# The skip term of eleven output blocks made by GpSimd: five of them leave TensorE, six leave VectorE

## The chip, the cores and the metric

The kernel runs on one core of a Trainium2 chip. The metric is the device time of one execution in microseconds (us). Three runs of the kernel before took 286.35, 286.96 and 289.43 us (median 286.96).

A core has these engines, each with its own queue of instructions in a fixed order: TensorE (PE: matmuls into the eight PSUM banks; the loads of its weights are shown as PEld), VectorE (DVE), ScalarE (ACT), GpSimd (POOL), and SyncE (SP), which here issues every DMA. An instruction whose inputs aren't there holds all that stand behind it on its engine.

## What is computed

x has 2048 tokens of 512 channels. The reference, cut to what matters here:

```python
g = _sigmoid((x * gate_w).sum(-1, keepdims=True))
a = _A_ref(x, A_wq, A_wk, A_wv, A_wo, A_beta)     # attention with memory, ends in o @ wo
b = _B_ref(x, B_A_re, ..., B_Dskip)               # y = ifft(fft(u) * fft(K)) + u * Dskip
return g * a + (1 - g) * b
```

So each output row is a sum of three terms: the attention output o times wo, the long convolution y, and the skip term x times a channel's constant (Dskip and the convolution's first tap). The kernel keeps (1 - g) apart as a scale for each token (omg4T) and has the rest of the gate inside o.

## The kernel before, in words

The whole program is a graph of operations. `op` records one with its engine, a function that emits it, and the tiles it reads and writes; `S.dma` records a DMA on SyncE, `S.evac` an eviction from PSUM that either ScalarE (L229, or L232 with a scale) or VectorE (L230, L233) can do. All matmuls go through one helper, L713, so the profile shows that line for all of them. `ORDER` (L382) is the written-out list of all operations: each entry is an operation's number, and behind slashes the buffer of each tile that this operation is the first to use; an "a" or "v" puts an eviction on ScalarE or VectorE. `replay` (L238) walks the list: each engine gets its operations in that order, and a tile that takes a buffer also takes, as `prev`, all users of the tile that had the buffer before. `emit` (L267) turns these into semaphore waits in front of the instruction. So both the place in the list and the buffer number decide what waits for what.

The tail of the program has three strands:

- The last attention heads: scores, an exponential by ScalarE (L1197, L1244), masks by VectorE (L1256), and a normalisation (L1158 to L1161). For token segments 0 to 2 a head group's result goes to DRAM and is read back transposed by SyncE (L1309; the last such read is oT2.3, operation 840). For segment 3, TensorE transposes it and it is evicted (oT3.3, on VectorE, L230); the eviction also waits for the read oT2.3 to land.
- The convolution (`conv`, L1413): for each of 32 frequencies a matmul, a product on VectorE (L1494), a matmul, an eviction to a V buffer (L1505, one of four) and a copy by DMA into V2 (L1506, "V copy" below). V copies 25, 26, 28, 29, 30 and 31 are the late ones.
- `finals` (L1510): sixteen output blocks b of 128 x 512, in a hand-mixed order.

A block's matmuls are fin (three of the four head groups' 128x512 matmuls), fir (one, half the convolution), fih (one, the fourth head group) and fis (one, the other half of the convolution). fih needs all four segments' fourth head group, oT2.3 and oT3.3 among them; fis needs all V copies.

- Blocks 8 to 15 keep their PSUM bank from fin to fis ("held"). Their skip term is part of fin: four matmuls of 128 columns of x against a diagonal matrix (L1532 to L1534). Their output is a scaled eviction by ScalarE (L232) or VectorE (L233): in this kernel 9 and 14 on VectorE, the others on ScalarE.
- Blocks 0 to 7 give the bank back. Their skip term is made on VectorE in an SBUF tile Ab (xD, L1528) from x rows that a DMA brings (xr0, xr2, xr4, xr6: one load for two blocks, 256 KB, two buffers); VectorE adds the first part of the sum (spl, L1550), and later the second part gives the output (out, L1564).

Two blocks share a store (L1567). TensorE takes the tail's matmuls in this order of blocks: fin1, fin6, fin7, fin10, fin3, fin5, fin0, fin2, fin8, fir8, fih8, fin11, fin14, fir14, fih10, fih14, fis14, fis8 and so on, between the last attention and convolution matmuls up to oT3.3; fin13 to fis13 end it. fih8 is the first fih.

SyncE's order there is: the load of wo, xr0, a convolution constant (CD29), xr6, a swap (X31), V copy 19, the read oT1.3, V copy 28, the other half of the swap, xr2, CD30, V copies 27, 20, 31, 26, the read oT2.3, xr4, V copies 25, 29, 30, then the eight stores.

Of the kernel before, what the change touches and what calls it, by code (L numbers as in the profile page):

```python
# [8 lines left out]
BF16 = mybir.dt.bfloat16  # L9
F32 = mybir.dt.float32  # L10
# [455 lines left out]
1687/0/1 1688a 1742 840 1682/0 1683/4/0 1006/2 1007 1776 1689/3 1008 1724/2 1727 1702/0 1703 1718/6 1690/1/3 1719
1026/5 1027v 1764/2 1765 1766 1780/5 1732/1 1657 1684a 1740/0 1743 1797/4 1685 1798 1777 1691a 1692 1799 1704 1800/0
1801v 1767/1 1733/1 1753/1 1721/0 1778/2 1769/7 1717/3 1720 1712/4 1713/3 1714 1722/4 1723 1768a 1779a 1728/2 1729
1770 1781 1782 1783 1784a 1734/6 1771 1772 1773v 1802/3 1803 1804 1785 1774 1754/5 1755 1735 1737/4 1730 1760/0 1761
1736 1705/5 1706 1707 1744/7 1745/2 1786/1 1762 1731 1715 1763 1805 1806a 1807 1787 1788 1789/1 1746 1738 1739 1791/6  # L470
# [71 lines left out]
def build_graph(nc, es, A_x, A_wq, A_wk, A_wv, A_wo, A_beta, B_A_re, B_A_im, B_B_re, B_B_im,  # L542
                B_C_re, B_C_im, B_log_dt, B_Dskip, gate_w, out):
    S = Sched(nc, es)
    ap = S.ap
    op = S.op
    x = A_x[0]
# [32 lines left out]
    G2T = cload(G2c, "G2", BF16, 60)  # L580
# [5 lines left out]
    diagT = S.keep(1024, BF16)  # L586
# [6 lines left out]
    omg4T = S.keep(64, F32)  # L593
# [53 lines left out]
    a = H2 + 16384  # L647
# [10 lines left out]
    a = T0  # L658
# [10 lines left out]
    a = H0  # L669
# [3 lines left out]
    a = H1  # L673
# [836 lines left out]
    def finals(V2, k0):  # L1510
        o3 = [oTp[(s_, hg)] for s_ in range(4) for hg in range(3)]
        o4 = [oTp[(s_, 3)] for s_ in range(4)]
        ou = None
        xr = {}
        for b4 in range(16):
            held = b4 not in SPILL
            S.key = k0 + b4
            P = S.ps()
            Ab = None if held else Tile(AbPs[SPILL[b4]], F32)
            if not held:  # L1520
                if b4 % 2 == 0:
# [6 lines left out]
                op("DVE", ("V1s", 512), lambda e, b4=b4, Ab=Ab, T=xr[b4]: e.scalar_tensor_tensor(  # L1528
                    ap(Ab, n=512), ap(T, (b4 % 2) * 512, n=512), ap(omg4T, b4, n=1), ap(DbT, n=512), ALU.mult, ALU.mult), r=[xr[b4], omg4T, DbT], w=[Ab], key=k0 - 10 + b4)
# [12 lines left out]
            def fv(e, P=None, b4=b4, q=0, last=False):
                return mm(e, ap(P, n=512), ap(G2T, q * 128, n=128), ap(V2[q], b4 * 512, n=512), False, last)
            S.tag = "fin%d" % b4
            op("PE", c_pe("F", 512), f1, r=o3 + (xTT + [woT, diagT] if held else [woT]), w=[P])
            S.tag = "fir%d" % b4
            op("PE", c_pe("F", 512), lambda e, P=P, fv=fv, held=held: fv(e, P, q=0, last=not held), r=[G2T, V2[0]], pw=[P])
            if not held:
                S.tag = "spl%d" % b4
                op("DVE", ("V1s", 512), lambda e, P=P, Ab=Ab, b4=b4: e.scalar_tensor_tensor(ap(Ab, n=512), ap(P, n=512), ap(omg4T, b4, n=1), ap(Ab, n=512), ALU.mult, ALU.add),  # L1550
                   r=[P, omg4T], w=[Ab])
                P = S.ps()
            S.tag = "fih%d" % b4
            op("PE", c_pe("F", 512), lambda e, P=P, f2=f2: f2(e, P), r=o4 + [woT], **({"pw": [P]} if held else {"w": [P]}))
            S.tag = "fis%d" % b4
            if b4 % 2 == 0:
                ou = Tile(ouP, BF16)
            op("PE", c_pe("F", 512), lambda e, P=P, fv=fv: fv(e, P, q=1, last=True), r=[G2T, V2[1]], pw=[P], acq=[ou])
            S.tag = "out%d" % b4
            dst = lambda ou=ou, b4=b4: ap(ou, (b4 % 2) * 512, n=512)  # L1560
            if held:
                S.evac(dst, lambda P=P: ap(P, n=512), 512, r=[P, omg4T], pw=[ou], scale=lambda b4=b4: ap(omg4T, b4, n=1))
            else:
                op("DVE", ("V1s", 512), lambda e, dst=dst, P=P, Ab=Ab, b4=b4: e.scalar_tensor_tensor(dst(), ap(P, n=512), ap(omg4T, b4, n=1), ap(Ab, n=512), ALU.mult, ALU.add),  # L1564
                   r=[P, omg4T, Ab], pw=[ou])
            if b4 % 2 == 1:
# [89 lines left out]
```

## Time and profile before

| | |
|---|---|
| profiled execution, its own time | 285.57 us |
| its span from first to last instruction | 283.8 us |
| granted TensorE clock, mean | 0.993 |
| VectorE instructions | 617, 93% of the span busy |
| ScalarE instructions | 320, 90% of the span busy |
| last GpSimd instruction | starts at 147.25 us |
| HBM traffic | 22.09 MB read, 7.86 MB written |

The profile is of one execution. Times in its rows are us from the span's start. A row of the timeline has the start, the time taken, the engine, the line, the operation and how many were merged; an "SPq" row is SyncE issuing a DMA, not the transfer. A row of a group has the busy time and the mean length in ns, and the engine's idle time ahead of it with what ended that. A row of windows gives, for one stretch, each engine's busy time, then the granted clock, the share of DMA engines in use and GB/s.

### The profile page before, as it was taken

What the parts mean: (1) busy time and instruction counts of PE and PEld (TensorE: products, weight loads), DVE (VectorE), ACT (ScalarE), POOL (GpSimd) and SP (SyncE); (2) the same over time, 40 slices, a digit from 0 to 9 for tenths busy, and PEclk for the clock granted to TensorE, in tenths of its full rate; (3) what the DMA queues carried; (4) which work ended last, traced back from release to release, by engine and by line L of the source; (5) the groups of instructions that cost most, each with busy time, mean ns of one, the idle gap of its engine ahead of it and who ended that gap; (6) DMA issues with size and microseconds to landing.
All of it is one profiled execution on the core that took longest, in us unless ns stands there. A gap on an engine that the chain in (4) does not pass through costs nothing.

```text
span 283.8 us, 9330 instructions
## 1 busy us (share of the span) xinstructions
PE 258.8 (91%) x3947; PEld 157.5 (56%) x3947; DVE 265.0 (93%) x617; ACT 254.3 (90%) x320; POOL 5.0 (2%) x10
## 2 busy tenths in 40 slices
PE   5778888887989899989999989999999999999995
PEld 2434454564656556756765657665555454556663
DVE  3999999999999999999999999999999999997774
ACT  5999999999999999999989999999999999994122
POOL 5000000000000000000000000000000000000000
PEclk9999899999999999999999999999999999999999
DMA  6997752422115346824743388588676786793415
GB/s 164 274 203 173 218 170 85 130 80 53 42 28 143 76 114 183 229 86 73 214 135 103 76 254 236 183 207 203 207 223 171 217 192 187 219 206 105 116 74 222
DMA packets 60187, 44.49 MB, mean 157 GB/s; under 512 B 36209, under 2 KB 53490, under 8 KB 60146
## 3 DMA queue, kind: packets, MB, share of 16 engines
q1 hardware_dynamic: 60146, 43.90, 57.4%
q8 instruction: 31, 0.51, 0.8%
q14 instruction: 10, 0.08, 0.1%
HBM read 22.09 MB, written 7.86 MB: 106 GB/s over the span
## 4 chain that ended last, share of the span: by engine, by line
ACT 43%; PE 41%; DVE 9%; issue 4%; DMA 2%; SPq 0%; ACTq 0%; DVEq 0%
PE psum L713 40%; ACT sb L1197 15%; ACT sb L229 13%; ACT sb L1244 8%; DVE sb L1353 3%; ACT sb L857 3%; ACT sb L865 2%; DVE sb L1362 1%; DVE sb L1356 1%; DMA scr_Z<-sb 1%; ACT sb L1028 1%; DMA sb<-c_ident 1%; ACT sb L1079 1%; DVE sb L1365 1%; ACT L935 0%
## 5 line engine op out<-in xcount | busy, mean ns | idle before, releaser
L713 PE MATMUL psum<-sb 128*128 128x17 bf16 (+18 forms) x3859 | 253.2, 230 | 16.4 <-ACT sb L1197 7.4
L713 PEld LDWEIGHTS psum<-sb 128*128 128x128 bf16 (+6 forms) x3859 | 152.3, 101 | 115.1 <-issue 19.3
L229 ACT ACTIVATE sb<-psum 128x512 bf16<-128x512 f32 (+4 forms) x155 | 87.7, 624 | 6.5 <-PE psum L713 5.8
L1244 ACT ACTIVATE sb<-psum 128x2048 bf16<-128x2048 f32 x40 | 75.9, 1899 | 2.2 <-PE psum L713 1.8
L1197 ACT ACTIVATE sb<-psum 128x2048 bf16<-128x2048 f32 (+1 forms) x40 | 70.0, 1751 | 2.3 <-PE psum L713 2.1
L1353 DVE TENSOR_TENSOR sb<-sb 128x4096 bf16<-128x4096 bf16 (+3 forms) x24 | 37.6, 1567 | 0.0
L230 DVE CAST sb<-psum 128x512 bf16<-128x512 f32 (+1 forms) x49 | 29.9, 625 | 1.2 <-PE psum L713 0.9
L1362 DVE TENSOR_TENSOR sb<-sb 128x512 bf16<-128x512 bf16 (+1 forms) x48 | 24.9, 534 | 0.1
L1256 DVE TENSOR_TENSOR sb<-sb 128x1024 bf16<-128x1024 bf16 (+1 forms) x40 | 22.5, 576 | 0.2
L1494 DVE TENSOR_TENSOR sb<-sb 128x1024 bf16<-128x1024 bf16 x32 | 21.5, 684 | 0.9 <-ACT sb L229 0.5
L1356 DVE TENSOR_TENSOR sb<-sb 128x2048 bf16<-128x2048 bf16 (+3 forms) x24 | 20.6, 859 | 0.0
L232 ACT ACTIVATE sb<-psum,sb 128x512 bf16<-128x512 f32 x6 | 4.0, 687 | 12.3 <-PE psum L713 12.3
L1161 DVE TENSOR_TENSOR sb<-psum,sb 128x256 bf16<-128x256 f32 x32 | 13.3, 415 | 0.3
L1365 DVE TENSOR_TENSOR sb<-sb 128x512 bf16<-128x512 bf16 (+1 forms) x24 | 12.7, 531 | 0.0
L857 ACT ACTIVATE sb<-sb 128x512 f32<-128x512 f32 x18 | 11.8, 659 | 0.0
L1158 DVE RECIPROCAL sb<-psum 128x16 f32<-128x16 f32 x32 | 7.8, 249 | 2.0 <-PE psum L713 1.8
L1298 DVE TENSOR_TENSOR sb<-psum,sb 128x512 bf16<-128x512 f32 x12 | 8.3, 689 | 0.2
L865 ACT ACTIVATE sb<-sb 128x512 bf16<-128x512 f32 x12 | 8.0, 683 | 0.0
L1079 ACT ACTIVATE sb<-sb 128x512 bf16<-128x512 bf16 x12 | 8.0, 662 | 0.0
L1028 ACT ACTIVATE sb<-psum 128x512 bf16<-128x512 bf16 x12 | 7.7, 645 | 0.0
L858 DVE TENSOR_TENSOR sb<-sb 128x256 f32<-128x256 f32 x18 | 7.4, 418 | 0.0
L859 DVE SCALAR_TENSOR_TENSOR sb<-sb 128x256 f32<-128x256 f32 x18 | 7.4, 417 | 0.0
(78 smaller groups left out, 121.8 us busy)
## 6 DMA issues: line engine op xcount, KB each, us to landing
sb<-sb SPq DMA_DIRECT2D x64, 128.0 KB, 3.2
sb<-c_DN SPq DMA_DIRECT2D x32, 224.0 KB, 3.1
scr_Z<-sb SPq DMA_DIRECT2D x16, 256.0 KB, 2.7
sb<-scr_Z SPq DMA_DIRECT2D x16, 256.0 KB, 3.7
sb<-in_A_x_dram SPq DMA_DIRECT2D x5, 512.0 KB, 4.7
sb<-c_DN SPq DMA_DIRECT2D x16, 160.0 KB, 3.4
out_dram<-sb SPq DMA_DIRECT2D x8, 256.0 KB, 2.0
scr_O<-sb SPq DMA_DIRECT2D x12, 128.0 KB, 3.1
```

The source lines that it names most:

```text
L229: fa = lambda e: e.activation(dst(), src(), ACT.Copy)
L230: fd = lambda e: e.tensor_copy(dst(), src())
L713: mm = lambda e, o_, l, r_, st, sp, **kw: e.matmul(o_, lhsT=l, rhs=r_, start=st, stop=sp, skip_group_check=True, **kw)
L857: op("ACT", ("As", 512), lambda e, sq=sq, Z=Z: e.activation(ap(sq, n=512), ap(Z, n=512), ACT.Square), r=[Z], w=[sq], key=PW[h] + PWS * k)
L1197: o = op("ACT", ("Ax", 4 * n), lambda e: e.activation(ap(pT, dims=[[512, 4], [1, n]]), ap(P, dims=[[512, 4], [1, n]]), ACT.Exp, scale=0.25 ...
L1244: o = op("ACT", ("Ax", 2048), lambda e, P=P, pT=pT: e.activation(ap(pT, n=2048), ap(P, n=2048), ACT.Exp, scale=0.25), r=[P], w=[pT])
L1256: op("DVE", ("V2", 128 * nb), lambda e, pT=pT, dims=dims: e.tensor_tensor(ap(pT, dims=dims + [[1, 128]]), ap(pT, dims=dims + [[1, 128]]), ...
L1353: op("DVE", ("V2n1" if n == 1 else "V2", 512 * n), lambda e: e.tensor_tensor(ap(tile, 2 * dst, [[2 * (sp - dst), 2], [2 * ne, 128], [1, 2 ...
L1356: op("DVE", ("V2n1" if n == 1 else "V2", 256 * n), lambda e: e.tensor_tensor(D_(), D_(), ap(tile, 2 * sp + ne * 128, [[-ne * 128, 2], [2 * ...
L1362: op("DVE", ("V2x" if sstep > 2 else "V2", 256 * n), lambda e, half=half: e.tensor_tensor(run(t2, n, 0, 1) if half else run(tile, ne, dst, ...
L1365: op("DVE", ("V2", 256 * n), lambda e: e.tensor_tensor(D_(), D_(), ap(t2, n * 128, [[-n * 128, 2], [2 * n, 64], [1, 2 * n]]), ALU.add), r= ...
L1494: op("DVE", ("V2", 1024), lambda e, Y=Y, XAB=XAB, K3=K3, Ke=Ke, xo=xo, u=u: e.tensor_tensor(ap(Y, dims=[[512, 2], [1, 512]]), ap(XAB, xo, ...
```

## The change

Five of the held blocks (`DSK`: 8, 9, 10, 11, 14) lose the four skip matmuls. Each gets a load of its own x rows (xq, 128 KB, from a new pool of four buffers) and an SBUF tile (new pool Abh). Their output becomes VectorE's add of PSUM times scale and the tile, as blocks 0 to 7 have it; ScalarE did it for 8, 10 and 11, VectorE for 9 and 14.

For these five and for blocks 2 to 7 (`GSK`, eleven in all) GpSimd makes the skip term with two instructions: xS multiplies x by the token's scale into f32, xM multiplies that in place by the channel's constant. Blocks 0 and 1 keep xD on VectorE. Blocks 12, 13 and 15 stay as they were. The pool of xr has four buffers in place of two.

The code also gains branches for splitting a last block in halves and for a store of one block, with `last = False` and `if False`; they make nothing here.

```diff
+DSK = (9, 14, 8, 10, 11,)
+GSK = (6, 7, 3, 14, 5, 8, 10, 2, 9, 11, 4,)
...
-    xrP = mkpool("xr", 2048, 2, 3)
+    xrP = mkpool('xr', 2048, 4, 3)
+    xqP = mkpool('xq', 1024, 4, 3)
...
+    a = H0
+    AbhP = mkpool('Abh', 2048, 6, 3)
...
+            skip = held and b4 not in DSK
...
+            elif not skip:
+                S.tag = "xq%d" % b4
+                T, xo = Tile(xqP, BF16), 0
+                S.dma(lambda T=T: ap(T, n=512), lambda b4=b4: bass.AP(x.tensor, x.offset + b4 * 512, [[8192, 128], [1, 512]]), 131072, w=[T])
+            if not skip and b4 in GSK:
+                S.tag = "xS%d" % b4
+                op("POOL", ("G", 512), lambda e, b4=b4, Ab=Ab, T=T, xo=xo: e.tensor_scalar(
+                    ap(Ab, n=512), ap(T, xo, n=512), ap(omg4T, b4, n=1), None, ALU.mult), r=[T, omg4T], w=[Ab])
+                S.tag = "xM%d" % b4
+                op("POOL", ("G", 512), lambda e, Ab=Ab: e.tensor_tensor(
+                    ap(Ab, n=512), ap(Ab, n=512), ap(DbT, n=512), ALU.mult), r=[DbT], w=[Ab])
...
-            if held:
-                S.evac(dst, lambda P=P: ap(P, n=512), 512, r=[P, omg4T], pw=[ou], scale=lambda b4=b4: ap(omg4T, b4, n=1))
...
+            elif skip:
+                S.evac(dst, lambda P=P: ap(P, n=512), 512, r=[P, omg4T], pw=[ohs[0], ou], scale=lambda b4=b4: ap(omg4T, b4, n=1))
```

The list `ORDER` is the same up to the load of wo (25); behind it the operations of `finals` have new numbers. From there (the part that matters):

```diff
+977 1035 978 983/3 1023 984a 1693/3 997/0/2 1024 1025 25/0 1752/1 1753/0 1754 1761/1 1762 998 1679/1 1700/0 1668/3
...
+1669/2/3 996/1 625 1716/0 1725/2 1726 1678 1756 1757 1012 1014/0/0 1763/0 1764 1790/3 999 1475 1670a 1000 1001 1727/2
+1728 1015 1662/4/2 1663a 1686/0 1815/0 1816/0 1817 1734/1 1743/0 1744 1671 1009/5 1013 1696/2 1765 1622 1770/0 1771/1
+1772 1787/0 1788/2 1789 1778/0 1717/3 1718 1779/3 1780 1697/6/3 1698a 1699 1664 1795/0 1796/4 1797 1735/1 1736 1005
+1016 1017 1018 1019/1 1745/7 1020 1021/1 1687/0/1 1688a 1746 840 1682/0 1683/4/0 1006/2 1007 1791 1689/3 1008 1729
```

The numbers to know:

| operation | number, buffer | operation | number |
|---|---|---|---|
| xr6, xr0, xr2, xr4 | 1752/1, 1700/0, 1716/0, 1734/1 | V copies 28, 27, 20 | 1678, 1671, 1622 |
| xq14, xq8, xq10 | 1815/0, 1770/0, 1787/0 | V copies 31, 26 | 1699, 1664 |
| xq9, xq11 | 1778/0, 1795/0 | read oT2.3 | 840 |
| xS8, xS10, xS9, xS11 | 1771, 1788, 1779, 1796 | V copies 25, 29, 30 | 1657, 1685, 1692 |

SyncE's order becomes: wo, xr6, CD29, xr0, half a swap, V copy 19, oT1.3, xr2, V copy 28, the other half of the swap, CD30, xq14, xr4, V copies 27 and 20, xq8, xq10, xq9, V copies 31 and 26, xq11, the read oT2.3, V copies 25, 29 and 30, the stores. GpSimd's order is blocks 6, 7, 3, 14, 5, 8, 10, 2, 9, 11, 4, xS and xM of each. The order of the matmuls on TensorE and of the other operations on VectorE is the same; out8, out10 and out11 join VectorE's.

More of the change, by code (lines that the diff above doesn't have):

```diff
@@ L466 @@
[L466 to L470, printed above, removed]
@@ L1542, in fv @@
-            def fv(e, P=None, b4=b4, q=0, last=False):
-                return mm(e, ap(P, n=512), ap(G2T, q * 128, n=128), ap(V2[q], b4 * 512, n=512), False, last)
+                        i = mm(e, ap(P[kc * 128 // w], kc * 128 % w, n=128), ap(xTT[0], kc * 2048 + b4, [[16, 128]]), ap(diagT, kc * 128, n=128), kc * 128 % w == 0, False)
+                for j, Pj in enumerate(P):
+                    for hg in range(3):
+                        i = mm(e, ap(Pj, n=w), ap(oTT[0], hg * 2048 + b4, [[16, 128]]), ap(woT, hg * 512 + j * w, n=w), hg == 0 and not skip, False)
@@ L1553, in finals @@
-            S.tag = "fih%d" % b4
-            op("PE", c_pe("F", 512), lambda e, P=P, f2=f2: f2(e, P), r=o4 + [woT], **({"pw": [P]} if held else {"w": [P]}))
-            S.tag = "fis%d" % b4
+                op("DVE", ("V1s", 512), lambda e, P=P, Ab=Ab, b4=b4: e.scalar_tensor_tensor(ap(Ab, n=512), ap(P[0], n=512), ap(omg4T, b4, n=1), ap(Ab, n=512), ALU.mult, ALU.add),
+                   r=[P[0], omg4T], w=[Ab])
+                P = [S.ps()]
             if b4 % 2 == 0:
                 ou = Tile(ouP, BF16)
-            op("PE", c_pe("F", 512), lambda e, P=P, fv=fv: fv(e, P, q=1, last=True), r=[G2T, V2[1]], pw=[P], acq=[ou])
+            ohs = [ou.part() for _ in range(2)]
```

74 lines of the change are left out of this document (51 added, 23 removed).

## The prediction, made before the changed kernel was run

> **What bounds the kernel now.** I read the page's share table first, then the end of the chain of waits, then the TensorE instructions of the last 12.5 us by shape, then SyncE's queue in order of time.
>
> ```profile
> PE 258.8 (91%) x3947; PEld 157.5 (56%) x3947; DVE 265.0 (93%) x617; ACT 254.3 (90%) x320; POOL 5.0 (2%) x10
> ```
>
> Three engines stand above 90%, so the mean decides nothing; GpSimd (POOL) is empty. The chain of waits ends with these rows (start, duration, engine, line):
>
> ```profile
> 248.28 32.26 PE psum L713 x261
> 280.53 0.02 issue
> 280.56 0.69 ACT sb L232
> ```
>
> From 248.3 to 280.5 us the end is set by 261 matmuls in one unbroken run. Other engines wait for TensorE there: ScalarE's scaled evictions (L232) below idle 12.3 us for it. What the change saves on TensorE here counts one to one, unless it makes TensorE wait.
>
> ```profile
> ACT sb L232 <- PE psum L713: 12.3, 4, 4.8
> ```
>
> The matmuls from 268.0 to 280.5 us by shape (busy us, mean ns of one), and one earlier run of eight:
>
> ```profile
> L713 PE MATMUL psum<-sb 128*128 128x512 bf16 x54 | 12.5, 380 | 0.0
> L713 PE MATMUL psum<-sb 128*128 128x128 bf16 x16 | 1.7, 226 | 0.0
> 18.21 1.90 PE L713 MATMUL psum<-sb 128*128 128x512 bf16 x8 [0.24 <-ACT sb L229]
> ```
>
> Matmuls overlap, so their mean length is no price. Eight 512-column ones take 1.90 us, of which the last is 0.38: a pitch of 1.52 / 7 = 0.217 us. Of 12.5 us, 54 x 0.217 = 11.7 are theirs, and 0.8 are left for 16 skip matmuls, 0.05 us each. The window's first two long ones began before it, so their pitch doesn't belong to it; with 52 it is 0.076. I take the middle, 0.063, so 0.25 us for the four of a block.
>
> SyncE's queue in this stretch (SPq):
>
> ```profile
> 244.25 0.43 SPq L225 DMA_DIRECT2D sb<-in_A_wo_dram  x1
> 244.73 0.51 SPq L225 DMA_DIRECT2D sb<-in_A_x_dram  x1
> 247.41 0.33 SPq L225 DMA_DIRECT2D sb<-c_DN  x1
> 247.78 0.44 SPq L225 DMA_DIRECT2D sb<-in_A_x_dram  x1
> 248.26 1.19 SPq L225 DMA_DIRECT2D sb<-sb  x2
> 249.49 1.26 SPq L1309 DMA_TRANSPOSE sb<-scr_O  x1
> 251.12 1.21 SPq L225 DMA_DIRECT2D sb<-sb  x2
> 252.37 0.58 SPq L225 DMA_DIRECT2D sb<-in_A_x_dram  x1
> 253.39 0.34 SPq L225 DMA_DIRECT2D sb<-c_DN  x1
> 254.66 6.26 SPq L225 DMA_DIRECT2D sb<-sb  x4
> 260.96 1.15 SPq L1309 DMA_TRANSPOSE sb<-scr_O  x1
> 262.15 0.58 SPq L225 DMA_DIRECT2D sb<-in_A_x_dram  x1
> 262.77 2.74 SPq L225 DMA_DIRECT2D sb<-sb  x3
> ```
>
> The row at 260.96 is the transposed read of oT2.3; the three at 262.77 are the last V copies (25, 29, 30). One engine issues all of these in order, and an issue that has to wait holds everything behind it.
>
> **The change part by part.** *TensorE loses* 20 skip matmuls: 5 x 0.25 = 1.25 us (bounds 5 x 0.2 and 5 x 0.3). All lie in the unbroken run. Blocks 10 and 8 come before fih8, blocks 11, 14 and 9 behind it: 0.50 and 0.75 us.
>
> *VectorE loses* six xD and gains three evictions from ScalarE (out8, out10, out11; out14 and out9 were its own and change their form).
>
> ```profile
> L1528 DVE SCALAR_TENSOR_TENSOR sb<-sb 128x512 f32<-128x512 bf16 x5 | 3.6, 746 | 0.0
> L1564 DVE SCALAR_TENSOR_TENSOR sb<-psum,sb 128x512 bf16<-128x512 f32 x8 | 5.5, 744 | 0.8 <-PE psum L713 0.8
> 264.95 0.69 DVE L230 CAST sb<-psum 128x512 bf16<-128x512 f32 x1 [0.41 <-PE psum L713]
> ```
>
> That is -6 x 0.75 + 3 x 0.74 = -2.3 us. It is worth nothing at the end, since the unbroken matmul run covers it; without that cover it would be a gain of at most 2.3. ScalarE's three evictions go the same way.
>
> *GpSimd gains* 22 instructions, xS and xM for eleven blocks. Its only rows:
>
> ```profile
> L995 POOL MEMSET sb<- 128x128 bf16 x4 | 2.5, 721 | 142.4 <-PE psum L713 142.4
> L990 POOL MEMSET sb<- 128x2176 bf16 x1 | 1.9, 1911 | 0.3 <-POOLq L1641 0.3
> L939 POOL MEMSET sb<- 128x544 f32 x1 | 0.9, 860 | 0.0
> ```
>
> The trace has no GpSimd arithmetic. The nearest row is the f32 fill of 544 columns, 0.86 us; the new ones write 512 f32 columns and read one or two operands besides. I bound one by p = 0.72 (the small fill) and 1.91 (the large one) and take 1.1, near 0.86 with a quarter for reading: 24 us in all, on an idle engine. The Trainium skill ("GPSIMD Engine Reference", section "Elementwise — side-by-side cycle accounting") gives about 2.6 cycles an element for two inputs at 1.2 GHz, and its section "Engine selection" calls one input roughly line-rate; by those, as an estimate, 1.11 us for xM and 0.43 for xS. No run here shows either, and the total by those prices would be 292.1 in place of the one below.
>
> *SyncE gains* five loads of 128 KB and two moved ones, and this decides. In the new list the five xq loads all take buffer 0, though the pool has four. So xq8 waits for xS14, xq10 for xS8, xq9 for xS10, xq11 for xS9: each a GpSimd instruction, each waiting at the head of SyncE's queue. Behind xq9 stand the V copies 31 and 26, behind xq11 the read of oT2.3 and the V copies 25, 29 and 30. Times to landing, first of the loads at 244.73 and 247.78 alone, then of all in 240 to 284 us:
>
> ```profile
> sb<-in_A_x_dram SPq DMA_DIRECT2D x1, 256.0 KB, 5.2
> sb<-in_A_x_dram SPq DMA_DIRECT2D x1, 256.0 KB, 3.4
> out_dram<-sb SPq DMA_DIRECT2D x8, 256.0 KB, 2.0
> sb<-sb SPq DMA_DIRECT2D x14, 128.0 KB, 2.4
> sb<-in_A_x_dram SPq DMA_DIRECT2D x4, 256.0 KB, 3.7
> sb<-scr_O SPq DMA_TRANSPOSE x3, 2.8
> ```
>
> For a 128 KB xq load I take L = 2.6, next to the 128 KB row (bounds 2.0 and 3.7). Then:
> - xr6 takes the issue at 244.73 and lands at 249.9; GpSimd makes blocks 6 and 7 until 249.9 + 4p = 254.3. xr0 takes the one at 247.78 and lands at 251.2.
> - xD0 and xD1 wait for xr0 and end at 251.2 + 2 x 0.75 = 252.7, when xr2 may be issued into their buffer. It lands 3.7 later: 256.4. Moved behind it are two copies and one constant (old issues 251.12 and 253.39), at most 1.6 us late; TensorE's wait below covers that, and uncovered it costs up to 1.6. xr4 waits for xS7 (249.9 + 3p = 253.2), hardly at all.
> - xS3, xM3, xS14 end at 256.4 + 3p = 259.7: xq8 is issued, lands at 262.3, while xM14, xS5, xM5 run to 263.0; xS8 ends at 264.1: xq10, landing at 266.7; xS10 ends at 267.8: xq9; xM10, xS2, xM2 run to 271.1, and xS9 ends at 272.2.
> - So xq11 is issued at 256.4 + 12p + L = 272.2, eleven us behind 260.96, and the read of oT2.3 at 272.6. It lands 2.8 later, and VectorE's eviction oT3.3, which waits for it, takes 0.69 (before: 264.95 to 265.64): fih8, the first matmul that needs both, starts at 276.1. Its old place is the start of this row (the matmuls that overlap 266.08 to 267.88 us; the first is fih8):
>
> ```profile
> 265.87 2.18 PE L713 MATMUL psum<-sb 128*128 128x512 bf16 x15
> ```
>
> All later matmuls stand behind fih8 in TensorE's fixed order: 276.1 - 265.9 = +10.2 us. The 0.50 us that blocks 10 and 8 save are swallowed by this wait.
>
> *What is late next.* V copy 30 is issued at 272.6 + 1.15 + 1.2 = 275.0 and lands at 277.4; fis14 needs it 2.2 us of matmuls behind fih8, at 278.3: hidden, by 0.9 us. xM4, GpSimd's last, ends at 272.2 + 2.6 + 4p = 279.2; it is for spl4, which frees a bank for fin13, the last block of TensorE's list, near 289: hidden.
>
> *The clock.* After ten us of waiting TensorE restarts. What that costs shows earlier in the trace (stretch, length, busy times, granted clock in the column behind POOL):
>
> ```profile
> 24.00:27.00 3.00, 1.77 (x35) 1.06 (x34) 2.44 (x12) 2.35 (x7) 0.00 (x0) 1.00 0.95 196
> 27.00:30.40 3.40, 3.17 (x19) 1.17 (x19) 3.40 (x13) 3.16 (x5) 0.00 (x0) 0.53 0.75 191
> ```
>
> Three us with TensorE only 59% busy were followed by 3.4 us at half clock. I take the same once: 3.4 / 2 = 1.7 us lost (bounds 0, if the gate doesn't fall, and 3.4, if it falls twice).
>
> **The sum** is +10.2 - 0.75 + 1.7 = +11.15 us on the profiled execution, 285.57: 296.7. That execution was 1.4 us faster than the median shown, 286.96, and inside the spread of the three runs, so a median may stand as much above the sum.
>
> **The rivals.** *A, the forecast:* SyncE held by the shared buffer. For it: the list's numbers. Its size is 12p + L; with p = 0.72 and L = 2.0 the read of oT2.3 is issued at 267.4 and the end is 291.5; with p = 1.5 and L = 2.8 it is 277.6 and 301.7; the far ends, p = 1.91 and L = 3.7, give 283.4 and 307.5.
>
> *B, the hold is short:* GpSimd makes one in 0.4 us. Then the loads are the longer part of the chain, 3L + 6p; with L = 2.0 xq11 goes out at 264.8, fih8 is 2.8 us late, and after so short a wait the clock may stay: 285.57 + 2.8 - 0.75 = 287.6. Against it: the smallest fill takes 0.72 us here, at a quarter of the columns.
>
> *C, the other side:* the waits at SyncE's head are over before 260.96, and the TensorE saving comes out whole: 285.57 - 1.25 = 284.3. It decides at xS9, which must end by 260.9, 4.5 us after xr2 lands; xq8, xq10 and xq9, one behind another, take 3 x 2.0 alone. So it needs the wait on the reused buffer to be missing, and the code puts the earlier users of a buffer in front of its next writer.
>
> *D, GpSimd and VectorE shut each other out:* a VectorE instruction with two SBUF operands and a GpSimd instruction that reads SBUF run one after the other. On GpSimd's chain between 256.4 and 264 stand these, four of 0.69:
>
> ```profile
> L1494 DVE TENSOR_TENSOR sb<-sb 128x1024 bf16<-128x1024 bf16 x3 | 2.1, 686 | 0.5 <-ACT sb L229 0.5
> L1256 DVE TENSOR_TENSOR sb<-sb 128x1024 bf16<-128x1024 bf16 x1 | 0.7, 681 | 0.0
> ```
>
> They would add 2.7 us, and xD0 behind xM6 another p: +3.8, so 300.5. Neither for nor against: GpSimd did nothing in this stretch. The Trainium skill ("SBUF — State Buffer", section "Who interferes with whom") states such an exclusive lock; no run here shows it.
>
> **How the numbers follow.** A 0.74, D 0.15, B 0.06, C 0.05. The time is A's, 296.7. The range runs from 290.5, A's low end with a us less of half clock, to 302.5, which holds A's 301.7 and D; B, C and the far ends of p and L stay outside, together under 2 in 10. One per cent, 2.9 us, is about what a measurement of this kernel can tell from no change. Slower by over that: A, D and a little of B, 0.90; within it: the rest of B and C, 0.08; faster 0.02.
>
> **What would show it.** Right: SyncE's x loads from 259 on spaced by 3 to 5 us, each issued as a GpSimd instruction ends; the read of oT2.3 issued near 272.6; one TensorE wait of about ten us near 265 and half clock behind it; GpSimd busy about 24 us. Wrong: a read of oT2.3 still near 261 (then C), GpSimd instructions under 0.5 us (B) or far over 1.5, VectorE's two-operand rows in 250 to 264 us grown or waiting for GpSimd (D), the clock staying full.

## The result and the profile after

The changed kernel takes 306.19 us (median of six runs, 302.0 to 310.76) against 286.4 (six runs, 285.25 to 289.43): the ratio is 1.0617, with a 95% interval of 1.0559 to 1.0674. Here and below a median is of all runs, while the ratio and its interval leave out those over 1.5% above the fastest of their kernel (here 306.63 and 310.76). The prediction was 296.7, range 290.5 to 302.5. The direction and the place were right, the size was not.

The profiled execution took 306.63 us, its span 304.8. The load of wo ends the part of the list that all kernels here share, yet the fourteen profiled executions issue it anywhere from 243.75 to 248.52 us: some lose a few us early. This one issues it at 247.20 where the one before did at 244.25, so 2.95 us are taken off below, and stretches are counted from that issue. From it to the end the kernel before took 283.8 - 244.25 = 39.55 us and the changed one 304.8 - 247.20 = 57.60: the change costs 18.05 us in these two executions, where 11.15 had been forecast.

The line numbers of the helper and of `finals` have moved: matmuls are L721, xS L1545, xM L1548, xD L1552, spl L1576, out L1608. First the page of the changed kernel, share table and four groups:

```profile
PE 262.8 (86%) x3927; PEld 158.3 (52%) x3927; DVE 265.2 (87%) x614; ACT 253.0 (83%) x317; POOL 37.1 (12%) x32
...
L721 PE MATMUL psum<-sb 128*128 128x17 bf16 (+16 forms) x3839 | 257.2, 232 | 34.1 <-DVE sb L230 15.6
...
L230 DVE CAST sb<-psum 128x512 bf16<-128x512 f32 (+1 forms) x49 | 29.8, 624 | 16.9 <-DMA sb<-scr_O 15.7
...
L1545 POOL TENSOR_SCALAR sb<-sb 128x512 f32<-128x512 bf16 x11 | 18.6, 1689 | 106.0 <-DMA sb<-in_A_x_dram 106.0
...
L1548 POOL TENSOR_TENSOR sb<-sb 128x512 f32<-128x512 f32 x11 | 13.7, 1241 | 0.9
```

The bound has changed its nature: the busy shares of TensorE, VectorE and ScalarE have all fallen, and one idle time stands out twice, 15.7 us of VectorE's eviction oT3.3 waiting for a read of scr_O (oT2.3), and 15.6 us of TensorE waiting for that eviction. TensorE's rows show the same wait as a hole in what had been one run:

```profile
264.21 6.75 PE L721 MATMUL psum<-sb 128*128 128x17 bf16 x50 [0.76 <-DVE sb L1264]
285.43 16.17 PE L721 MATMUL psum<-sb 128*128 128x512 bf16 x72 [14.46 <-DVE sb L230]
```

The row at 285.43 begins with fih8; before, fih8 started at 265.87. Less the 2.95 us it is 16.6 us late. Why the read is late stands in SyncE's rows (the x3 row is xq8, xq10 and xq9, the x1 at 281.51 is xq11):

```profile
247.20 0.43 SPq L225 DMA_DIRECT2D sb<-in_A_wo_dram  x1
...
252.65 1.47 SPq L1317 DMA_TRANSPOSE sb<-scr_O  x1
256.73 0.35 SPq L225 DMA_DIRECT2D sb<-in_A_x_dram  x1
...
265.61 10.68 SPq L225 DMA_DIRECT2D sb<-in_A_x_dram  x3
...
281.51 0.33 SPq L225 DMA_DIRECT2D sb<-in_A_x_dram  x1
281.89 1.14 SPq L1317 DMA_TRANSPOSE sb<-scr_O  x1
```

and in GpSimd's: xS14 ends at 265.58, xS9 at 281.48, and 0.03 us behind each a load goes out.

```profile
260.50 1.56 POOL L1545 TENSOR_SCALAR sb<-sb 128x512 f32<-128x512 bf16 x1 [1.11 <-DMA sb<-in_A_x_dram]
262.14 1.46 POOL L1548 TENSOR_TENSOR sb<-sb 128x512 f32<-128x512 f32 x1
263.58 2.00 POOL L1545 TENSOR_SCALAR sb<-sb 128x512 f32<-128x512 bf16 x1
265.67 1.69 POOL L1548 TENSOR_TENSOR sb<-sb 128x512 f32<-128x512 f32 x1
267.34 2.08 POOL L1545 TENSOR_SCALAR sb<-sb 128x512 f32<-128x512 bf16 x1
...
270.65 1.56 POOL L1545 TENSOR_SCALAR sb<-sb 128x512 f32<-128x512 bf16 x1
272.29 1.15 POOL L1548 TENSOR_TENSOR sb<-sb 128x512 f32<-128x512 f32 x1
274.37 1.56 POOL L1545 TENSOR_SCALAR sb<-sb 128x512 f32<-128x512 bf16 x1 [0.93 <-DMA sb<-in_A_x_dram]
...
279.92 1.56 POOL L1545 TENSOR_SCALAR sb<-sb 128x512 f32<-128x512 bf16 x1
```

Each of the two instructions shows two lengths: 1.56 us (xS) and 1.15 (xM) undisturbed, from 270.65 on, where VectorE waits; up to 2.08 and 1.69 ahead of that, where VectorE works. VectorE's side of it is the row of xD0 and xD1, 2.31 us for two that took 1.41 before:

```profile
254.39 2.31 DVE L1552 SCALAR_TENSOR_TENSOR sb<-sb 128x512 f32<-128x512 bf16 x2 [0.62 <-DMA sb<-in_A_x_dram]
```

Last the stretches of the changed kernel; the granted clock is the number before the DMA share:

```profile
272.00:280.00 8.00, 0.00 (x0) 0.00 (x0) 0.00 (x0) 0.60 (x1) 6.82 (x7) 0.77 0.23 66
280.00:284.00 4.00, 0.00 (x0) 0.00 (x0) 0.00 (x0) 0.00 (x0) 2.66 (x3) 0.50 0.25 65
284.00:290.00 6.00, 4.58 (x11) 1.80 (x12) 2.01 (x3) 0.00 (x0) 5.39 (x4) 0.50 0.22 66
290.00:304.00 14.00, 11.59 (x62) 6.77 (x60) 10.06 (x15) 2.02 (x3) 0.00 (x0) 0.99 0.41 151
```

The last matmul ahead of the wait ends at 270.96. A mean of 0.77 over 272 to 280, if the clock goes straight from full to half, puts the fall near 276.3, some 5 us into the wait; the clock stays there until near 290, over 4 us behind the restart. The matmuls that start from 285.43 to 289.70 are 0.43 us apart, in place of 0.216 from 290.5 on: ten gaps, 2.1 us lost.

### The profile page after: what moved, and what is told of

The parts are those of the page before. It is cut to its first block, busy times and chain, and to the rows that moved or that the text cites. A ratio compares the mean times of both kernels' runs of the same rounds, so it can differ in the third digit from the quotient of the medians.

```text
span 304.8 us, 9316 instructions
## 1 busy us (share of the span) xinstructions
PE 262.8 (86%) x3927; PEld 158.3 (52%) x3927; DVE 265.2 (87%) x614; ACT 253.0 (83%) x317; POOL 37.1 (12%) x32
## 4 chain that ended last, share of the span: by engine, by line
PE 40%; ACT 26%; DVE 14%; DMA 8%; POOL 6%; issue 3%; SPq 2%; ACTq 0%; DVEq 0%
PE psum L721 39%; ACT sb L1205 12%; ACT sb L229 8%; POOL sb L1545 4%; DMA sb<-in_A_x_dram 3%; DVE sb L1361 3%; SPq L225 2%; POOL sb L1548 2%; DVE sb L1370 2%; DMA sb<-c_DN 2%; DVE sb L230 2%; ACT sb L865 2%; DVE sb L1364 1%; ACT sb L873 1%; ACT sb L1252 1%
## 5 line engine op out<-in xcount | busy, mean ns | idle before, releaser
L721 PE MATMUL psum<-sb 128*128 128x17 bf16 (+16 forms) x3839 | 257.2, 232 | 34.1 <-DVE sb L230 15.6
L721 PEld LDWEIGHTS psum<-sb 128*128 128x128 bf16 (+6 forms) x3839 | 152.6, 101 | 136.1 <-issue 26.8
L230 DVE CAST sb<-psum 128x512 bf16<-128x512 f32 (+1 forms) x49 | 29.8, 624 | 16.9 <-DMA sb<-scr_O 15.7
L1545 POOL TENSOR_SCALAR sb<-sb 128x512 f32<-128x512 bf16 x11 | 18.6, 1689 | 106.0 <-DMA sb<-in_A_x_dram 106.0
L1003 POOL MEMSET sb<- 128x128 bf16 x4 | 2.5, 721 | 145.1 <-PE psum L721 145.1
L232 ACT ACTIVATE sb<-psum,sb 128x512 bf16<-128x512 f32 x3 | 2.0, 687 | 20.5 <-PE psum L721 20.5
L1548 POOL TENSOR_TENSOR sb<-sb 128x512 f32<-128x512 f32 x11 | 13.7, 1241 | 0.9
L1169 DVE TENSOR_TENSOR sb<-psum,sb 128x256 bf16<-128x256 f32 x32 | 13.2, 413 | 0.3
L1373 DVE TENSOR_TENSOR sb<-sb 128x512 bf16<-128x512 bf16 (+1 forms) x24 | 12.7, 529 | 0.0
L1608 DVE SCALAR_TENSOR_TENSOR sb<-psum,sb 128x512 bf16<-128x512 f32 x13 | 8.9, 742 | 4.3 <-PE psum L721 4.3
```

The costliest lines, as they stand in the source:

```text
L230: fd = lambda e: e.tensor_copy(dst(), src())
L721: mm = lambda e, o_, l, r_, st, sp, **kw: e.matmul(o_, lhsT=l, rhs=r_, start=st, stop=sp, skip_group_check=True, **kw)
L1545: op("POOL", ("G", 512), lambda e, b4=b4, Ab=Ab, T=T, xo=xo: e.tensor_scalar(ap(Ab, n=512), ap(T, xo, n=512), ap(omg4T, b4, n=1), None, AL ...
L1548: op("POOL", ("G", 512), lambda e, Ab=Ab: e.tensor_tensor(ap(Ab, n=512), ap(Ab, n=512), ap(DbT, n=512), ALU.mult), r=[DbT], w=[Ab])
```

## The experiments

Theory 1 is the forecast with other sizes: SyncE is held by loads that wait for GpSimd, and GpSimd's length sets how long. Its rivals were that the reused buffer costs by itself, that the half clock is what is lost, and, once these were answered, three smaller costs under the big one: GpSimd and VectorE holding each other up, the order of the loads, and the loads themselves. Orders are given by the operations' names, with the buffer behind a slash.

| kernel | median us (runs) | ratio, 95% interval | load of wo to end | wo to read of oT2.3 |
|---|---|---|---|---|
| before | 286.4 (6) | | 39.55 | 16.71 |
| changed | 306.19 (6) | 1.0617, 1.0559 to 1.0674 | 57.60 | 34.69 |
| 1 own buffers | 293.06 (4) | 1.0211, 1.0151 to 1.0271 | 44.88 | 19.88 |
| 2 short xM | 298.27 (4) | 1.0378, 1.0307 to 1.0449 | 51.70 | 28.43 |
| 3 filler matmuls | 303.32 (4) | 1.0583, 1.0506 to 1.0661 | 55.78 | 32.90 |
| 4 read ahead of the loads | 301.27 (4) | 1.0510, 1.0444 to 1.0575 | 53.99 | 19.03 |
| 5 xS and xM swapped | 302.76 (2) | 1.0576, 1.0494 to 1.0659 | 54.90 | 31.62 |
| 6 five only, late loads | 288.57 (12) | 0.9989, 0.9944 to 1.0035 | 40.38 | 16.92 |
| 7 five only, early loads | 289.11 (12) | 1.0068, 1.0026 to 1.0110 | 41.17 | 18.77 |
| 8 GpSimd's work alone | 287.64 (12) | 1.0068, 1.0026 to 1.0110 | 40.85 | 17.76 |
| 9 the loads alone | 287.58 (12) | 1.0060, 1.0021 to 1.0100 | 40.89 | 18.08 |
| 10 five only, middle | 288.05 (12) | 1.0059, 1.0021 to 1.0097 | 41.53 | 18.03 |
| 11 six only | 290.86 (6) | 1.0162, 1.0105 to 1.0218 | 43.56 | 20.11 |
| 12 six only, old order | 290.67 (6) | 1.0149, 1.0087 to 1.0210 | 42.54 | 17.34 |

The ratio is to runs of the kernel before made beside each kernel; their medians are 286.82 (kernels 1, 2, 3, 6), 286.49 (4, 5, 7, 11) and 286.61 (8, 9, 10, 12). The last two columns are of one profiled execution each, and how much they vary between executions of one kernel was not measured, so differences of about 1 us there are hints.

**1. A buffer for each of the five loads.** It takes away what makes the loads wait.

```diff
-    xrP = mkpool('xr', 2048, 4, 3)
-    xqP = mkpool('xq', 1024, 4, 3)
+    xrP = mkpool('xr', 2048, 2, 3)
+    xqP = mkpool('xq', 1024, 5, 3)
...
-xq8/0 xq10/0 xq9/0 xq11/0
+xq8/1 xq10/2 xq9/3 xq11/4
```

> The changed kernel with a buffer of its own for each of the five xq loads (five buffers, the pool of xr back at two); nothing else differs. Theory 1 (SyncE is held by the reused buffer, and GpSimd's own length comes next): the read of oT2.3 is issued near 261 to 263 again and fih8 starts near 266 to 267, so the 14.6 us wait of TensorE goes. GpSimd's 22 instructions then run nearly without a break from 250 to 284 (2.77 us a pair and some contention), spl2, out11 and spl4 wait for them, and the end is 6 to 8 us later than before: 291 to 294 us, ratio 1.02 to 1.03. Rival 2 (the hold was the whole cost): 285 us, ratio 0.995. Rival 3 (the reused buffer is not the cause, GpSimd slows VectorE in general): 300 us or more, ratio over 1.045, with the read of oT2.3 still late.

Measured 293.06. The four loads go out without waiting, and the longest wait for GpSimd is now at an output:

```profile
260.05 1.44 SPq L225 DMA_DIRECT2D sb<-in_A_x_dram  x3
...
265.68 0.47 SPq L225 DMA_DIRECT2D sb<-in_A_x_dram  x1
266.20 1.14 SPq L1317 DMA_TRANSPOSE sb<-scr_O  x1
```

```profile
DVE sb L1608 <- POOL sb L1548: 3.3, 1, 3.3
```

Of the 18.05 us, 57.60 - 44.88 = 12.7 come from the shared buffer. Of the 5.3 that are left, 3.2 stand ahead of the read of oT2.3 (19.88 - 16.71) and 2.2 behind it. Both were a question for the later runs. The last thing that oT3.3 waits for is no longer that read but TensorE (1.1 us).

**2. xM on 16 of 512 columns.** It leaves out the multiplication by the channel's constant on the other 496, and makes GpSimd shorter with everything else in place.

```diff
-                    ap(Ab, n=512), ap(Ab, n=512), ap(DbT, n=512), ALU.mult), r=[DbT], w=[Ab])
+                    ap(Ab, n=16), ap(Ab, n=16), ap(DbT, n=16), ALU.mult), r=[DbT], w=[Ab])
```

> The changed kernel, but xM multiplies only 16 of its 512 columns by the channel's constant; the other 496 keep x times the token's scale. Theory 1 (the wait is the chain of GpSimd instructions and loads behind xr2): five xM of 1.15 to 1.7 us stand in the chain to xq11 and shrink to about 0.2, less what the loads then show, so the read of oT2.3 is issued 5 to 6 us earlier and the kernel takes 5 to 6 us less than the changed one: 298 us, ratio 1.04. Rival 3 (contention in general): as much less as VectorE's instructions get shorter, under 2 us.

```profile
L1548 POOL TENSOR_TENSOR sb<-sb 128x16 f32<-128x16 f32 x11 | 2.4, 218 | 0.9
```

Measured 298.27, as expected. Five xM on the chain are each 0.9 to 1.5 us shorter, and the read of oT2.3 goes out 34.69 - 28.43 = 6.3 us earlier. GpSimd's price is what the read waits for.

**3. Sixty matmuls of 512 columns ahead of fir8**, to keep TensorE busy in the wait.

```diff
+                for _ in range(60 if b4 == 8 else 0):
+                    mm(e, ap(P[0], n=512), ap(ident, n=128), ap(woT, n=512), True, False)
```

> The changed kernel with 60 more matmuls of 512 columns at the head of fin8, about 13 us of TensorE's wait, whose results the first real matmul overwrites. If the half clock behind the wait is a cost of the wait (theory 1), the ten matmuls from fih8 to fis14 run at 0.216 us and not 0.43 us, and the end comes 2.0 to 2.5 us earlier than in the changed kernel: 301.5 us, ratio 1.053. If the clock is not ruled by TensorE's idle time, or the filler itself delays fih8, no gain or a loss.

```profile
272.00:280.00 8.00, 8.00 (x38) 3.64 (x38) 0.07 (x1) 0.60 (x1) 6.63 (x6) 1.00 0.33 87
280.00:284.00 4.00, 3.95 (x19) 2.24 (x19) 1.94 (x3) 0.00 (x0) 3.83 (x4) 1.00 0.29 92
284.00:290.00 6.00, 6.00 (x31) 3.47 (x30) 4.42 (x7) 0.00 (x0) 0.86 (x1) 1.00 0.00 0
```

The clock stays at 1.00, and the median is 2.9 us lower, but the intervals overlap, and in the profile the read is issued 1.8 us earlier, which is all of its gain: from the end of oT3.3 to the end are 300.1 - 280.62 = 19.5 us here and 304.8 - 285.37 = 19.4 in the changed kernel. The reason is in the matmuls of 512 columns behind the end of oT3.3, first in this kernel (280.8 to 297), then in the changed one (285.4 to 302):

```profile
L721 PE MATMUL psum<-sb 128*128 128x512 bf16 x70 | 15.8, 379 | 0.1
L721 PE MATMUL psum<-sb 128*128 128x512 bf16 x60 | 15.9, 424 | 14.5 <-DVE sb L230 14.5
```

There are ten more here: the end of what stands ahead of fih8 ran on past oT3.3, for 10 x 0.216 = 2.2 us, about the 2.1 us that the half clock takes from the changed kernel. So the sixty were too many to show a gain, and the half clock costs some 2 of the 18 us.

**4. The read of oT2.3 ahead of the loads.** The loads keep their shared buffer and their waits; only what stands behind them is gone.

```diff
-xq8/0 xq10/0 xq9/0 V31 V26 xq11/0 oT2.3 V25 V29 V30
+V31 V26 oT2.3 V25 V29 V30 xq8/0 xq10/0 xq9/0 xq11/0
```

> The changed kernel with one difference: in the list, the loads xq8, xq10, xq9 and xq11, with the GpSimd work that stands behind them, come behind V copy 30 instead of ahead of V copies 31 and 26 and of the read of oT2.3. All five loads still share buffer 0, and each still waits for a GpSimd instruction. Theory 1 (what costs is what stands behind a waiting load in SyncE's order): the read of oT2.3 is issued near 262, fih8 starts within 2 us of its place before (265.9), and TensorE's wait of 14.6 us there is gone. The loads go out at about 265.5, 269, 273 and 278.5, GpSimd ends near 286, so a smaller wait appears later, of VectorE for GpSimd in front of out10, out11 and spl4: 293.06 of the kernel with own buffers plus about 3.5, since GpSimd ends that much later, is 296.5 us (294 to 299). Rival (the waits on the reused buffer cost by themselves, wherever they stand): the time stays at 305 to 307.

```profile
267.04 1.16 SPq L1317 DMA_TRANSPOSE sb<-scr_O  x1
268.24 5.61 SPq L225 DMA_DIRECT2D sb<-sb  x3
273.89 13.78 SPq L225 DMA_DIRECT2D sb<-in_A_x_dram  x4
```

```profile
280.16 1.52 PE L721 MATMUL psum<-sb 128*128 128x512 bf16 x6 [1.37 <-DVE sb L1608]
286.62 5.36 PE L721 MATMUL psum<-sb 128*128 128x512 bf16 x19 [4.95 <-DVE sb L1576]
```

The rival is refuted as far as the 14.5 us wait goes: it is gone with the buffer still shared, and the time lies under the rival's 305 to 307. Neither forecast held the time, though. The oT3.3 starts at 273.28, 25.3 us behind the load of wo and not 20.7 as before, held by TensorE, where fih8 within 2 us of its place had been expected. The 296.5 was missed by 4.8 us: the loads now wait behind V copy 30, whose issue ends at 273.85 here and not at 265.5 (3.76 us of that are of the early part, the load of wo being issued at 248.01), so GpSimd ends at 295.3, and the wait has moved to the outputs (TensorE waits for spl, L1576, and out, L1608).

**5. The two GpSimd instructions in the other order**: first x times the channel's constant by tensor_tensor, then the token's scale by tensor_scalar, in place.

```diff
-e.tensor_scalar(Ab, x, omg4T[b4], None, mult)
-e.tensor_tensor(Ab, Ab, DbT, mult)
+e.tensor_tensor(Ab, x, DbT, mult)
+e.tensor_scalar(Ab, Ab, omg4T[b4], None, mult)
```

> The changed kernel with the two GpSimd instructions of a block in the other order: first x (bf16) times the channel's constant (bf16) by tensor_tensor into f32, then the token's scale in place on f32 by tensor_scalar. Tells what made xS 1.56 us alone where xM took 1.15. If it is the form (one tensor and a scalar for each partition): tensor_scalar stays near 1.56 alone and tensor_tensor near 1.15. If it is the bf16 tensor in an f32 product: the first becomes the longer, 1.5 or more, and the second falls to about 1.1. A pair takes about 2.7 us either way, the chain to xq11 is nearly the same, and the time is 304 to 307 us.

```profile
L1548 POOL TENSOR_SCALAR sb<-sb 128x512 f32<-128x512 f32 x11 | 18.2, 1652 | 1.1
L1545 POOL TENSOR_TENSOR sb<-sb 128x512 f32<-128x512 bf16 x11 | 13.2, 1197 | 104.2 <-DMA sb<-in_A_x_dram 104.2
```

It is the form: the one with a scalar for each partition is the longer in either place and with either type of input, and undisturbed the two take 1.56 and 1.15 us again. The time is a little under the expected 304 to 307, with two runs only.

**6. The five held blocks alone.** The six other blocks go back to xD on VectorE, SyncE's order is that of before, and the five loads, each with its own buffer, stand behind V copy 20; xD4 and xD2 are moved ahead of out14, and out8 and out10 right behind fis10.

```diff
-GSK = (6, 7, 3, 14, 5, 8, 10, 2, 9, 11, 4,)
+GSK = (14, 8, 10, 11, 9)
...
 V20
+xq14/0 xq8/1 xq10/2 xq11/3 xq9/4
```

> The kernel before with the skip term of the same five held blocks made by GpSimd, each xq load in a buffer of its own and all five issued behind V copy 20, where SyncE is idle; blocks 2 to 7 stay with VectorE's xD. xD4 and xD2 stand ahead of out14, and out8 and out10 right behind it. Theory 1: GpSimd needs five pairs, 14 us from about 258.5, each just ahead of its eviction; nothing holds SyncE; the saving of 20 skip matmuls shows as 0.5 to 1.25 us: 285.2 to 286 us, ratio 0.996 to 0.998. If GpSimd's contention with VectorE's two-operand instructions matters by itself, a loss of 1 to 3 us.

```profile
DVE sb L1607 <- POOL sb L1547: 2.0, 1, 2.0
```

Most of the loss is gone, but no gain is seen: 0.9989, with 1 inside the interval; the median of all twelve runs is 288.57 beside 286.82, so a loss of half a per cent isn't excluded. An output still waits 2.0 us for GpSimd, which starts 16.1 us behind the load of wo. So the next kernel starts it earlier.

**7. The same with the loads right behind xr0.**

```diff
 xr0
+xq14/0 xq8/1 xq10/2 xq11/3 xq9/4
 CD29
 xr6
+xS14 xM14 xS8 xM8 xS10 xM10 xS11 xM11 xS9 xM9
```

> The five held blocks alone on GpSimd, as in the kernel with five only (six xD on VectorE, a buffer for each of five loads), but the five loads are issued right behind xr0, near 245, where SyncE idles for 2.2 us, and GpSimd's ten instructions follow from about 249 to 263. Theory 1 (the saved skip matmuls are worth their 1.25 us when nothing waits for GpSimd): 286.8 - 1.25 = 285.6 us, ratio 0.996 (0.992 to 0.999), with no VectorE wait for GpSimd. Rival 1 (GpSimd beside VectorE's two-operand instructions slows VectorE and the convolution that goes through it): the time is the same or up to 2 us longer, ratio 1.000 to 1.007, with TensorE waits for VectorE between 249 and 265. Rival 2 (the loads delay xr6, the constant and the copies behind them): TensorE waits near 250, 1 to 2 us longer.

First xD and the masks of the kernel before from 248 to 266 us, then the same two here:

```profile
L1528 DVE SCALAR_TENSOR_TENSOR sb<-sb 128x512 f32<-128x512 bf16 x6 | 4.4, 746 | 0.0
L1256 DVE TENSOR_TENSOR sb<-sb 128x1024 bf16<-128x1024 bf16 (+1 forms) x5 | 2.8, 576 | 0.0
```

```profile
L1551 DVE SCALAR_TENSOR_TENSOR sb<-sb 128x512 f32<-128x512 bf16 x5 | 4.9, 1004 | 0.0
L1263 DVE TENSOR_TENSOR sb<-sb 128x1024 bf16<-128x1024 bf16 (+1 forms) x5 | 4.5, 916 | 0.0
```

```profile
PE psum L720 <- DMA sb<-c_DN: 1.1, 1, 1.1
PE psum L720 <- DVE sb L1263: 0.7, 1, 0.7
```

Theory 1's 1.25 us don't come out: the kernel is slower, by 0.3 to 1.1%. VectorE no longer waits for GpSimd, but TensorE waits for CD29 and for VectorE. Both rivals show: xD takes 1.00 us in place of 0.75 and the masks 0.92 in place of 0.58 between 248 and 266 us. The next two kernels price them one by one.

**8. GpSimd's work alone** in the kernel before: ten instructions that nothing uses.

```diff
+for g in range(5):
+    e.tensor_scalar(Ag, woT, omg4T[g], None, mult)
+    e.tensor_tensor(Ag, Ag, DbT, mult)
```

> The kernel before, with ten GpSimd instructions added that nothing uses: five times the pair of the change, on columns of wo in place of x, free to run from the landing of wo near 249 to about 263, without any load. Everything else does the work that it did. Tells apart why the kernel with the five loads early was not faster. Theory (GpSimd holds VectorE's two-operand instructions up): TensorE waits for VectorE between 249 and 263, and the read of oT2.3 goes out later: 1.5 to 3 us longer, ratio 1.005 to 1.010. Rival (the loads ahead of the constant and xr6 did it): ratio 1.000 (0.997 to 1.003).

```profile
L1558 DVE SCALAR_TENSOR_TENSOR sb<-sb 128x512 f32<-128x512 bf16 x5 | 4.5, 920 | 0.0
L1263 DVE TENSOR_TENSOR sb<-sb 128x1024 bf16<-128x1024 bf16 (+1 forms) x5 | 4.0, 806 | 0.0
...
L1582 DVE SCALAR_TENSOR_TENSOR sb<-psum,sb 128x512 f32<-128x512 f32 x4 | 3.0, 748 | 0.2
```

Ratio 1.0068 (1.0026 to 1.0110), 1.3 us longer from the load of wo to the end; the medians of all runs, 287.64 and 286.61, are 1.0 us apart. So work that no one waits for costs about as much as the 1.25 us that the change was to save, though the size is uncertain. The xD and the masks, with both operands in SBUF, have grown; the spl (L1582), with one in PSUM, takes 0.748 as before. Not every row with two has grown: the convolution's product takes 0.680 in kernels 7 and 8 (0.685 before). In kernel 10 it is the other way round, the product takes 0.798 and xD 0.744.

**9. The loads alone**, which nothing uses.

```diff
 xr0
+q0/0 q1/1 q2/2 q3/3 q4/4
 CD29
```

> The kernel before, with the five loads of 128 KB right behind xr0 added, that nothing uses; no GpSimd work. The other half of the kernel with the five loads early. If the loads delay the constant CD29, xr6 and the swap: a TensorE wait of about 1 us for CD29 near 250, ratio 1.003 to 1.006. If GpSimd alone made the difference: ratio 1.000 (0.997 to 1.003).

```profile
PE psum L720 <- DMA sb<-c_DN: 1.1, 1, 1.1
```

Ratio 1.0060 (1.0021 to 1.0100), 1.3 us in the profile; the medians of all runs, 287.58 and 286.61, are 1.0 us apart. SyncE needs 3.75 us to issue xr0 and the five, so CD29 is issued 4.27 us behind the load of wo in place of 3.16, and it takes 4.4 us to land in place of 3.1. Together: -1.25 + 1.30 + 1.34 = +1.4 us for kernel 7, which measured 41.17 - 39.55 = 1.6. That fits, but the 1.25 is the prediction's estimate, which no run shows by itself.

**10. The loads behind CD30**, where VectorE is no longer full.

```diff
 CD30
+xq14/0 xq8/1 xq10/2 xq11/3 xq9/4
 V27
```

> The five held blocks alone on GpSimd again, with the five loads behind CD30, where GpSimd's ten instructions begin near 256, behind the stretch in which VectorE has no idle time, and end near 270, ahead of most of the outputs that need them. Theory: the saved 1.25 us come out but for what GpSimd costs VectorE's few two-operand instructions there: ratio 0.996 to 1.000, about 286 us. Rival (the loads, 2.2 us of issuing, and GpSimd delay the late V copies): ratio 1.002 to 1.008.

```profile
PE psum L720 <- DVE sb L1607: 1.6, 1, 1.6
```

Slower by 0.2 to 1.0%: the rival. The read of oT2.3 goes out 1.3 us later, and TensorE waits for a bank that an output (L1607) gives back. None of three places for the five gave a gain, so no version that beats the kernel before was found.

**11. The six other blocks alone**, all skip matmuls back on TensorE, the changed kernel's order of the loads.

```diff
-DSK = (9, 14, 8, 10, 11,)
-GSK = (6, 7, 3, 14, 5, 8, 10, 2, 9, 11, 4,)
+DSK = ()
+GSK = (6, 7, 3, 5, 2, 4)
```

> The other part alone: blocks 2 to 7 on GpSimd in the order 6, 7, 3, 5, 2, 4, all skip matmuls back on TensorE, no xq loads, evictions where the kernel before has them. GpSimd takes 6 x 2.77 = 16.6 us and ends near 268, before spl2 and spl4 need it. Theory 1 (this part costs and brings nothing, since nothing waits for GpSimd and VectorE has slack): ratio 1.000 (0.996 to 1.004), about 286.8 us. Rival (the two engines hold each other up, as the 1.65 us of xD1 showed, and xr2 goes out late): 1 to 3 us longer, ratio 1.004 to 1.010.

```profile
253.96 1.15 SPq L1316 DMA_TRANSPOSE sb<-scr_O  x1
258.82 0.35 SPq L225 DMA_DIRECT2D sb<-in_A_x_dram  x1
```

```profile
256.09 2.70 DVE L1551 SCALAR_TENSOR_TENSOR sb<-sb 128x512 f32<-128x512 bf16 x2 [1.01 <-DMA sb<-in_A_x_dram]
```

Here is the second hold on SyncE: it idles from 255.11 to 258.82 with xr2 at its head, until xD1 ends at 258.79, and V copy 28, half a swap and CD30 stand behind xr2. xr0 had been moved behind CD29, so xD0 starts later, and the pair takes 2.70 us beside GpSimd in place of 1.41. The read of oT2.3 goes out 3.4 us later: the 3.2 us that kernel 1 had left. The hold delays more than the read: a product of the convolution waits 1.8 us for a copy (1.9 in kernel 1, none before), and oT3.3 then waits last for TensorE, not for the read.

**12. The six alone with SyncE's order as before.**

```diff
-xr6/1 CD29 xr0/0
+xr0/0 CD29 xr6/1
...
-oT1.3 xr2/0 V28 X31 CD30
+oT1.3 V28 X31 xr2/0 CD30
```

> Blocks 2 to 7 alone on GpSimd, as in the kernel with six only, but SyncE's order of all loads and copies, and two xr buffers, as in the kernel before; GpSimd's instructions stand in the list where the xD stood. Theory (of the 4 us that the kernel with six only was longer from the load of wo to the end, most comes from SyncE: xr0 behind the constant CD29 and xr2, which waits for xD1, ahead of V copy 28, the swap and CD30): the read of oT2.3 is issued at most 1 us later after the load of wo than before, ratio 1.000 to 1.006, about 287.5 us. Rival (the two engines holding each other up make the whole difference): the ratio stays near 1.016.

```profile
DVE sb L1575 <- POOL sb L1547: 7.8, 3, 3.5
```

The read of oT2.3 is back, 0.6 us behind its place before, so the order of the loads was its cause, together with what it brings about: xD0 and xD1 now run ahead of GpSimd's first instruction and take 1.40 us. The time is not back: xr6 now comes second, GpSimd starts 7.7 us behind the load of wo instead of 5.5, and three spl wait 7.8 us in all for it. One wait stands in the other's place. With either order the six cost 1.5%; an order free of both wasn't tried.

## Why the prediction failed, step by step

**The mechanism was right.** The four loads went out as GpSimd instructions ended, the read of oT2.3 right behind xq11, one long wait of TensorE ahead of fih8, half clock behind it. Kernel 1 shows that the shared buffer makes 12.7 of the 18.05 us, and kernel 4 that its long wait comes through SyncE's order.

**The step that failed** is GpSimd's price: "The nearest row is the f32 fill of 544 columns, 0.86 us ... I bound one by p = 0.72 ... and 1.91 ... and take 1.1". A fill was a poor stand-in for arithmetic. From xS3's start at 260.50 to xq11 at 281.51 are 21.0 us, where 12p + L was 15.8. On this chain stand five pairs at 2.775 us (two of them from 274.37 to 279.92) and two more xS at 1.56, 17.0 us undisturbed in place of 13.2 (+3.8). xM3, xS14, xM14 and xS5 are longer than undisturbed by 0.31, 0.44, 0.54 and 0.52 (+1.8). One load is on the chain, xq10, 2.16 us from the end of xS8 to the start of xS10, in place of 2.6 (-0.4). The mean price of all 22, 32.3 / 22 = 1.47 us, is inside the bounds; the value taken inside them was wrong.

**Rival D was true as well**, and it was not a rival but an addition: besides the 1.8 us on the chain it has most of xr2's 1.1 us (issued 9.53 us behind wo, forecast 8.45), since xD0 and xD1 took 2.31 us together in place of 1.5; xr0's landing was 0.2 us late too. So 3.8 + 1.8 + 1.1 - 0.4 = 6.3 us of the 6.4 by which fih8 came later than forecast. The Trainium skill ("SBUF — State Buffer", section "Who interferes with whom") says that a VectorE instruction with two SBUF inputs and a GpSimd instruction that reads SBUF contend, and that one with at most one SBUF input doesn't, outside VectorE's two-port modes. The rows of kernels 7 and 8 agree where xD (two inputs) went from 0.75 to 0.92 and 1.00 and spl (one) stayed at 0.748; the product, with two and unchanged there, shows that not every such instruction is the one that waits.

**The skill's price.** The Trainium skill ("GPSIMD Engine Reference", sections "Elementwise — side-by-side cycle accounting" and "Engine selection") gave 1.11 us for xM by estimate, and 1.15 was measured. The Trainium skill's "1-input is roughly line-rate" gave 0.43 for xS by estimate, and 1.56 was measured, in f32 as in bf16 (kernel 5); there the measurement decides.

**The clock.** From fih8 to the end the changed kernel took 1.44 us longer than before (304.8 - 285.43 against 283.8 - 265.87). With the forecast's -0.75 for the skip matmuls that leaves 2.2 us for half clock, where 1.7 was forecast. The ten gaps at half clock (2.1 us) and kernel 3 (2.2 us) give the same size. The Trainium skill ("TensorE: Matmul & The Clock Gate", section "What's actually happening") tells of free-running windows of about 3.4 us, one idle window to fall and one busy to rise; a fall some 5 us into the wait and a rise over 4 us after it fit with that.

**The order of the loads**, "at most 1.6 us late; TensorE's wait below covers that, and uncovered it costs up to 1.6", was covered, as said. Uncovered it is 3.2 to 3.4 us (kernels 1 and 11), twice the bound: I had priced the instructions that xr2 is moved ahead of, and not xr2's own wait for xD1, which GpSimd's work makes longer.

**What was right at nothing** was right only under the long wait. VectorE's fewer instructions, the loads and GpSimd's work "on an idle engine" were given no price of their own; alone, the work and the loads cost 1.0 to 1.3 us each (kernels 8 and 9), together more than the 1.25 at which the skip matmuls were priced.

**The sum.** 296.7 + 6.4 (fih8) + 0.5 (behind it) + 2.95 (the early part of this execution) = 306.55, and 306.63 was measured. The range's upper end, 302.5, held the higher price or the contention, and both came; even without the early part the sum is 303.6.

## What to carry to other kernels

An engine that stands at 2% is not free: price its instruction by a measured one of the same form, and ask whose instructions grow beside it. A load that reuses a buffer puts its waiting on the queue that issues it, so look at what stands behind it there before its bytes; a buffer for each of the five loads took away 12.7 of 18 us here. When two rivals are mechanisms that don't exclude each other, the range has to hold their sum.

## What the hardware showed that I had not expected

- GpSimd's tensor_scalar with a scalar for each partition takes 1.56 us for 128x512 into f32, a tensor_tensor of that size 1.15: one tensor less to read, and longer.
- GpSimd lengthens VectorE's work with which it has no data in common: ten instructions that nothing waits for cost 1.0 to 1.3 us of 286 (kernel 8), and GpSimd's own grow too, from 1.56 to 2.08 us and from 1.15 to 1.69.
- Five loads of 128 KB that nothing uses, put where SyncE idled for 2.2 us, cost 1.0 to 1.3 us (kernel 9): they take over 3 us to issue, and the constant behind them is issued 1.1 us later and takes 1.3 us longer to land.
